# Three loads of 128 rows issued as 121 rows and 7 rows

## The chip, the cores and the metric

The kernel runs on one core of one Trainium2 chip. The metric is device time in microseconds of one execution, the median over several. A core has five engines, each with its own instruction queue: TensorE (PE, matmuls, with its weight loads PEld), VectorE (DVE), ScalarE (ACT), GpSimd (POOL) and SyncE (SP), which here only issues transfers. Transfers are carried out by 16 DMA engines. TensorE writes to eight PSUM banks, and the other engines copy the results out.

## What is computed

Sigmoid attention over 8 batches of 12 heads, 448 positions and 64 columns, then a token-mixing MLP over the joined heads:

```python
scores = scale * np.matmul(q, k.transpose(0, 1, 3, 2)) - np.log(S)
attn = 1.0 / (1.0 + np.exp(-scores))
attn_out = np.matmul(attn, v)
x = attn_out.transpose(0, 2, 1, 3).reshape(B, S, H * D)
wq, wk = x @ w_q, x @ w_k
W_tok = scale * np.einsum('bsd,btd->bst', wq, wk)
mixed = np.einsum('bst,btd->bsd', W_tok, x)
out = np.maximum(mixed, 0.0) @ w_out
```

q, k and v are float32 in HBM, 11 MB each; the output is 11 MB.

## The kernel before

The 12 heads of a batch are taken four at a time, a *quad*, so there are 24 quads, numbered in order. One quad needs one load each of q, k and v: a float32 tile of 128 rows by 896 columns, 448 KB. For v, and for q and k of some quads, a row is two pieces of 1792 B; for q and k of the other quads of the first 14 it is one piece of 3584 B. Each tile is cast to bf16 (mostly on POOL: `cast1`, lines 201, 218 and 224), q and k are brought into transposed order (on PE, or by POOL copies in `arrange`, lines 163 to 169, and DVE transposes, lines 254 to 285), and then come per quad seven score blocks on PE (line 328), seven sigmoids on ACT (line 333) and seven value blocks on PE (line 350). The MLP of a batch follows its three quads and is interleaved with later quads.

The order is written out by hand. A string `PLAN` has one letter for each step of PE with what hangs on it. A list `ORDER` has the order of the loads, and of the casts that follow them. Around the three loads in question it reads

```python
"... k4 q4 v2 w0 k5 q5 w1 v3 W5 v4 q6 k6 w4 k7 v5 q7 v6 q8 k8 k9 q9 v7 q10 v8 k10 ..."
```

(`k5` is k of quad 5; `w0` is the load of the MLP's first weights, and the other `w` entries stand for weights that load through POOL's queue.) `pump_loads` issues the loads on SP's queue in this order, each into one of eight float32 tiles of the pool `ld`, as soon as the program's order of casts has released the tile eight loads back. `pump` and `cast_now` do the casts in the same order on POOL, one after the other. So a cast whose load has not landed holds all of POOL behind it. `load_wout` issues two loads of the output weights on POOL's own DMA queue, between the casts.

Besides what the tiles need, each transfer from SP's queue waits for a transfer issued before it on the same of eight completion counters (`DMAHW0` to `DMAHW7`), which go round in turn. In this place that is the one eight transfers back.

Lines that matter below: 171 to 194 (`load1`: the two `dma_start`, profiled as lines 177 and 188), 201 (cast of q or k into the arranged order), 218 (cast of v), 278 and 254 (DVE transposes of q and k), 302 to 316 (DVE copies out of the PE transposes), 401 (a DVE copy of the MLP's input), 670 (the output weights).

Of the kernel before, what the change touches and what calls it, by code (L numbers as in the profile page):

```python
# [17 lines left out]
def kernel(  # L18
# [17 lines left out]
    P = 128  # L36
    NI, NP = 7, 64
# [112 lines left out]
    SRC = dict(q=q, k=k, v=v)  # L150
# [3 lines left out]
    def arrange(n, eng):  # L154
# [12 lines left out]
        for g in range(2):  # L167
            lo = slice(64 * g, 64 * g + 32)
            eng.tensor_copy(out=w[lo, 1], in_=z[lo])  # L169

    def load1(n, nm, eng):
        u, j = quads[n]
        if KIND[n] in "cer" and nm != "v":
            t = p_ld.tile([P, 2 * RUN + PAD], F32, tag="ld", name=nm + "32")
            t = t[:, 0 : 2 * RUN] if n < SPLIT else t.rearrange("p (y x) -> p y x", y=2)[:, :, 0:RUN]
            rows = SRC[nm][u, 4 * j : 4 * j + 4]
            eng.dma_start(
                out=t,
                in_=rows.rearrange("h (p r) d -> (h p) (r d)", r=2 * NI)
                if n < SPLIT else rows.rearrange("h (p y r) d -> (h p) y (r d)", y=2, r=NI),  # L180
            )
            ld[nm, n] = (
                t.rearrange("p (y i e d) -> p e y i d", y=2, i=NI, e=2)
                if n < SPLIT else t.rearrange("p y (i e d) -> p e y i d", i=NI, e=2)
            )
            return
        t = p_ld.tile([P, 2, NI * HD], F32, tag="ld", name=nm + "32")
        eng.dma_start(
            out=t,
            in_=SRC[nm][u, 4 * j : 4 * j + 4].rearrange(  # L190
                "(g h) (p i) d -> (h p) g (i d)", g=2, i=NI
            ),
        )
        ld[nm, n] = t

# [486 lines left out]
    def cols(r):  # L682
# [9 lines left out]
        out=ident, in_=ident, compare_op=ALU.not_equal, fill=1.0, base=0,  # L692
# [35 lines left out]
    def pump_loads():  # L728
        while len(loaded) < len(ORDER):

            late = len(ring) > LATE
            if late and not allowed[0]:
                break
            nm, n = ORDER[len(loaded)]
            if nm == "w" and n or (nm, n) in CASTING:
                loaded.add((nm, n))
                continue
            if len(ring) >= 8 and ring[-8] not in cast:
                break
            allowed[0] -= late  # L740
            ring.append((nm, n))
            if nm == "w":
                load_weights()
            else:
                load1(n, nm, nc.sync)
            loaded.add((nm, n))
# [81 lines left out]
    for t in PLAN:  # L828
# [17 lines left out]
        elif kind == "P":  # L846
            n, i = divmod(c, NI)
# [17 lines left out]
        elif t == "z":  # L865
            n = quads_r.pop(0)
# [16 lines left out]
        elif kind == "M":  # L883
            u, x = divmod(c, NC // 2)
# [48 lines left out]
```

## Time and profile before

| What | Time or share |
|---|---|
| median of 3 runs | 182.57 us |
| lowest and highest run | 180.17 and 185.29 us |
| span of the profiled execution | 180.1 us |
| ACT, line 333, the sigmoids | 140.0 us busy, 168 of them, 948 ns each |
| PE, line 328, the scores | 62.2 us busy |
| PE, line 350, the values | 47.3 us busy |
| POOL, line 201, casts of q and k | 43.2 us busy, 36 of them |
| mean rate of all transfers | 263 GB/s |

The span goes from the first to the last instruction of one execution, the one that was profiled; nothing further of that execution's own time is given, and the runs are other executions. The slices on the profile's page are 1/40 of the span, about 4.5 us each; a digit is a busy share in tenths. In the lists of waits a row names the engine and line that waited, what it waited for, the total in microseconds, how often, and the longest. In the rows on single tiles the three numbers are minimum, median and maximum; "DMA to landing" is the time from the issue of a transfer until all its data has arrived. In rows of the chain and of a timeline the first number is the start and the second the duration.

### The profile page before, as it was taken

To read this page: it belongs to the slowest core of one execution; us is meant where nothing else is said; L and a number is where in the kernel's file an instruction comes from. 1 tells how busy PE (TensorE), PEld (TensorE's weight loads), DVE (VectorE), ACT (ScalarE), POOL (GpSimd) and SP (SyncE) were. 2 spreads that over 40 slices of the span, in tenths; PEclk is the share of its full clock that TensorE was granted. 3 is DMA by queue.
4 is the path that set the end of the run, shared out by engine and by line. 5 is a ranking of instruction groups with operands and counts; after the bars stand their busy time and mean duration, and the time that the engine had idled before them with its cause. 6 is when DMAs were issued, how large, how long until landed. Compare 5 with 4: busy or idle time off the path is not lost.

```text
span 180.1 us, 7907 instructions
## 1 busy us (share of the span) xinstructions
PE 169.6 (94%) x3440; PEld 112.2 (62%) x3440; DVE 145.6 (81%) x227; ACT 159.0 (88%) x208; POOL 121.4 (67%) x166
## 2 busy tenths in 40 slices
PE   7698899889899999999999999999999999999990
PEld 3334445444575555445667786678887788888660
DVE  3578899997989896889999999979898886768351
ACT  4699999999899999999999999999999989976300
POOL 1028799689999999999999999979979910010000
PEclk9999999999999999999999999999999999999999
DMA  5999999999999998899998889987795523505876
GB/s 177 355 372 349 322 383 381 280 302 356 342 294 349 339 265 267 217 319 365 343 300 315 217 288 305 342 322 213 200 338 173 135 64 73 137 4 122 201 208 175
DMA packets 27475, 47.31 MB, mean 263 GB/s; under 512 B 3888, under 2 KB 23600, under 8 KB 27440
## 3 DMA queue, kind: packets, MB, share of 16 engines
q1 hardware_dynamic: 26160, 44.64, 78.0%
q0 software_dynamic: 800, 1.18, 3.6%
q10 hardware_dynamic: 480, 0.98, 1.5%
q8 instruction: 27, 0.44, 1.0%
q14 instruction: 8, 0.07, 0.1%
HBM read 35.78 MB, written 11.01 MB: 260 GB/s over the span
## 4 chain that ended last, share of the span: by engine, by line
PE 56%; POOL 16%; DMA 15%; DVE 5%; ACT 2%; issue 2%; SPq 1%; POOLq 0%
PE banks L539 15%; PE banks L350 10%; PE banks L328 10%; PE banks L620 8%; DMA q<-in_q_dram 6%; POOL qk L201 5%; DMA w<-in_moe_w_k_dram 4%; DMA k<-in_k_dram 3%; POOL qk L169 3%; DMA wout<-wout 2%; ACT at L333 2%; POOL v L218 2%; PE banks L579 2%; PE banks L413 2%; POOL swap L163 2%
## 5 line engine op out<-in xcount | busy, mean ns | idle before, releaser
L333 ACT ACTIVATE at<-banks 128x896 bf16<-128x896 f32 x168 | 140.0, 948 | 3.4 <-PE banks L328 3.0
L328 PE MATMUL banks<-qk 64*64 64x448 bf16 x672 | 62.2, 358 | 3.3 <-ACT at L333 1.6
L350 PE MATMUL banks<-at,v 64*64 64x448 bf16 x672 | 47.3, 351 | 0.8 <-ACT at L333 0.7
L328 PEld LDWEIGHTS <-qk 64*64 64x64 bf16 x672 | 25.9, 105 | 20.7 <-issue 13.2
L539 PE MATMUL banks<-wout,mx 64*64 64x384 bf16 x672 | 36.6, 323 | 0.0
L201 POOL CAST qk<-k 128x896 bf16<-128x896 f32 x19 | 22.8, 1199 | 10.6 <-DVE qk L302 9.7
L350 PEld LDWEIGHTS <-v 64*64 64x64 bf16 x672 | 23.2, 107 | 8.6 <-issue 1.7
L539 PEld LDWEIGHTS <-mx 64*64 64x64 bf16 x672 | 23.3, 107 | 4.5 <-issue 0.5
L359 DVE CAST xt<-banks 128x896 bf16<-128x896 f32 x22 | 23.8, 1083 | 2.3 <-PE banks L350 1.8
L620 PE MATMUL banks<-wout,mx 128*128 128x384 bf16 (+1 forms) x138 | 24.4, 320 | 0.0
L480 DVE TENSOR_SCALAR mx<-banks 128x1024 bf16<-128x1024 f32 (+3 forms) x22 | 21.3, 972 | 1.9 <-PE banks L493 0.7
L201 POOL CAST qk<-q 128x896 bf16<-128x896 f32 x17 | 20.4, 1198 | 2.6 <-DMA q<-in_q_dram 1.3
L218 POOL CAST v<-v 128x896 bf16<-128x896 f32 x22 | 20.6, 950 | 1.4 <-DMA v<-in_v_dram 0.4
L620 PEld LDWEIGHTS <-mx 128*128 128x128 bf16 x138 | 12.3, 98 | 9.8 <-issue 3.2
L285 DVE STREAM_TRANSPOSE qk<-qk 128x448 f32<-128x448 f32 x28 | 17.0, 627 | 0.4 <-POOL qk L166 0.3
L163 POOL COPY swap<-qk 32x448 uint32<-32x448 uint32 x28 | 15.5, 554 | 2.3 <-DVE qk L201 0.7
L166 POOL COPY qk<-qk 32x448 uint32<-32x448 uint32 x28 | 15.8, 566 | 1.6
L169 POOL COPY qk<-swap 32x448 uint32<-32x448 uint32 x28 | 15.8, 564 | 1.6
L254 DVE STREAM_TRANSPOSE qk<-qk 32x448 f32<-32x448 f32 x24 | 15.3, 636 | 0.6
L422 POOL COPY wq<-wqk 64x448 bf16<-64x448 bf16 x3 | 1.7, 555 | 15.7 <-DVE wqk L421 15.7
L653 DVE COPY o<-banks 128x384 f32<-128x384 f32 x12 | 6.6, 553 | 5.7 <-PE banks L620 5.3
L653 ACT COPY o<-banks 128x384 f32<-128x384 f32 x9 | 4.4, 490 | 7.1 <-PE banks L620 6.9
(91 smaller groups left out, 206.5 us busy)
## 6 DMA issues: line engine op xcount, KB each, us to landing
q<-in_q_dram SPq DMA_DIRECT2D x24, 448.0 KB, 6.6
v<-in_v_dram SPq DMA_DIRECT2D x24, 448.0 KB, 6.3
k<-in_k_dram SPq DMA_DIRECT2D x23, 448.0 KB, 7.0
out_dram<-o SPq DMA_DIRECT2D x50, 192.0 KB, 3.9
wout<-in_moe_w_out_dram POOLq DMA_DIRECT2D x2, 576.0 KB, 12.2
wout<-wout SPq DMA_DIRECT2D x12, 96.0 KB, 6.2
out_dram<-o ACTq DMA_DIRECT2D x4, 192.0 KB, 3.5
k<-in_k_dram SPq DMA_DIRECT2D x1, 256.0 KB, 5.6
```

The source lines that it names most:

```text
L163: eng.tensor_copy(out=z[lo], in_=w[hi, 0])
L169: eng.tensor_copy(out=w[lo, 1], in_=z[lo])
L201: COPY[e](out=f[:, :, "qk".index(nm)].rearrange("p e i d y -> p e y i d"), in_=ld.pop((nm, n)),)
L218: COPY[e](out=t16.rearrange("p b i d -> p (b i d)"), in_=ld.pop((nm, n)).rearrange("p b x -> p (b x)"),)
L285: nc.vector.transpose(out=qk[n][:, t].rearrange("p t i n -> p (t i n)").bitcast(F32), in_=w)
L328: nc.tensor.matmul(sc[HALF[h], g, 0:S], qk[n][HALF[g], h, 1, i, :], qk[n][HALF[g], h, 0].rearrange("p i n -> p (i n)"), start=True, stop=True,
L333: inst = nc.scalar.activation(at, sc[:, :, 0:S], ACTF.Sigmoid, bias=attn_bias, scale=attn_scale)
L350: nc.tensor.matmul(ps[HALF[g], h, 0:S], ld["v16", n][HALF[h], g, i, :], ats[n, i][HALF[h], g, :], start=(i == 0), stop=(i == NI - 1),)
L359: read(fb, COPY[eng](out=xt(u, j)[:, :, 0:S], in_=ps[:, :, 0:S]))
L480: inst = nc.vector.tensor_scalar(dst, ps, moe_scale, 0.0, ALU.mult, ALU.max)
L539: nc.tensor.matmul(ps[HALF[x], y, 0:NB], mx[HALF[y], u, b, 64 * (i - 3 * y) : 64 * (i - 3 * y) + 64], wout16[HALF[y], slot(y, b), x * NB : ...
L620: nc.tensor.matmul(ps, mxs[w][:, 2 * S * c + m * P : 2 * S * c + (m + 1) * P], wout16[:, c, w0:w1], start=(c == 0), stop=(c == NC - 1),)
```

## The change

A helper `load_rows` issues a load as it was, or, if it is one of `k5`, `v5` and `v6`, as two transfers: rows 0 to 120, then rows 121 to 127. Tiles, casts, `PLAN` and `ORDER` stay as they are.

```diff
+    THIN = "k5 v5 v6".split()
+    CUT = 121
+
+    def load_rows(nm, n, eng, dst, rows):
+
+        if f"{nm}{n}" not in THIN:
+            eng.dma_start(out=dst, in_=rows)
+            return
+        for r in (slice(0, CUT), slice(CUT, P)):
+            eng.dma_start(out=dst[r], in_=rows[r])
+
     def load1(n, nm, eng):
...
-            eng.dma_start(
-                out=t,
-                in_=rows.rearrange("h (p r) d -> (h p) (r d)", r=2 * NI)
+            load_rows(
+                nm, n, eng, t,
+                rows.rearrange("h (p r) d -> (h p) (r d)", r=2 * NI)
                 if n < SPLIT else rows.rearrange("h (p y r) d -> (h p) y (r d)", y=2, r=NI),
             )
...
-        eng.dma_start(
-            out=t,
-            in_=SRC[nm][u, 4 * j : 4 * j + 4].rearrange(
-                "(g h) (p i) d -> (h p) g (i d)", g=2, i=NI
-            ),
+        load_rows(
+            nm, n, eng, t, SRC[nm][u, 4 * j : 4 * j + 4].rearrange("(g h) (p i) d -> (h p) g (i d)", g=2, i=NI),
         )
```

SP's queue from v of quad 5 to q of quad 9, before; a row has the line, the tile written and its source, the shape, and what it waits for (`DMAHW` are the eight completion counters):

```order
L188 DMA v_444<-in_v_dram 128x2x448 [waits DMAHW7_49,Pool_49]
L177 DMA q_478<-in_q_dram 128x896 [waits DMAHW0_49,Pool_49]
L188 DMA v_481<-in_v_dram 128x2x448 [waits DMAHW1_49,Pool_49]
L177 DMA q_486<-in_q_dram 128x896 [waits DMAHW2_49,Pool_49]
L177 DMA k_504<-in_k_dram 128x896 [waits DMAHW3_49,Pool_49]
L177 DMA k_662<-in_k_dram 128x896 [waits DMAHW4_49,Pool_49]
L177 DMA q_666<-in_q_dram 128x896 [waits DMAHW5_49,Pool_49]
```

The same place after:

```order
L180 DMA v_445<-in_v_dram 121x2x448 [waits DMAHW0_49,Pool_49]
L180 DMA v_445<-in_v_dram 7x2x448 [waits DMAHW1_49]
L177 DMA q_480<-in_q_dram 128x896 [waits DMAHW2_49,Pool_49]
L180 DMA v_483<-in_v_dram 121x2x448 [waits DMAHW3_49,Pool_49]
L180 DMA v_483<-in_v_dram 7x2x448 [waits DMAHW4_49]
L177 DMA q_489<-in_q_dram 128x896 [waits DMAHW5_49,Pool_49]
L177 DMA k_507<-in_k_dram 128x896 [waits DMAHW6_49,Pool_49]
L177 DMA k_665<-in_k_dram 128x896 [waits DMAHW7_49,Pool_49]
L177 DMA q_669<-in_q_dram 128x896 [waits DMAHW0_49,Pool_49]
```

Two transfers more stand there. The last row, q of quad 9, waited for counter 5, last used by q of quad 6; it now waits for counter 0, last used by the 121 rows of v of quad 5.

POOL's queue at the casts of quad 7 before (line 434 is a copy of the MLP, line 163 begins `arrange`):

```order
L434 COPY wq_119<-wqk_117 64x448 [waits DVE_49,Pool_49]
L201 CAST qk_781<-k_438 128x2x2x224 [waits DMAHW6_49,Pool_49]
L218 CAST v_785<-v_444 128x896 [waits DMAHW7_49,PE_49]
L201 CAST qk_781<-q_478 128x2x2x224 [waits DMAHW0_49]
L163 COPY swap<-qk_781 32x448 [waits Pool_49]
```

And after; the lines below the helper stand 8 further down in the file:

```order
L442 COPY wq_119<-wqk_117 64x448 [waits DVE_49,Pool_49]
L209 CAST qk_784<-k_439 128x2x2x224 [waits DMAHW7_49,Pool_49]
L226 CAST v_788<-v_445 128x896 [waits DMAHW1_49,DMAHW0_49,PE_49]
L209 CAST qk_784<-q_480 128x2x2x224 [waits DMAHW2_49]
L163 COPY swap<-qk_784 32x448 [waits Pool_49]
```

The instructions and their order are the same; the cast of v of quad 5 waits for two counters in place of one.

## The prediction

> **What bounds the kernel now.** I read the page first, for shares and slices, then the busy time by stretches around the three loads, then the waits in the same place, the chain of waits, and the landing times of single loads.
>
> ```profile
> span 180.1 us, 7907 instructions
> ...
> PE 169.6 (94%) x3440; PEld 112.2 (62%) x3440; DVE 145.6 (81%) x227; ACT 159.0 (88%) x208; POOL 121.4 (67%) x166
> ...
> DMA  5999999999999998899998889987795523505876
> ...
> q1 hardware_dynamic: 26160, 44.64, 78.0%
> ...
> q8 instruction: 27, 0.44, 1.0%
> ```
>
> TensorE is busy 94% of the span, and DMA is at nine tenths or more for the first 70 us. The last line shows 27 instruction packets of 0.44 MB / 27 = 16 KB; each took 0.010 x 16 x 180.1 / 27 = 1.07 us. A packet lies on one DMA engine alone, so some engine is later than its fifteen neighbours. The rows do not say which one.
>
> ```profile
> 24.00:30.00 6.00, 5.85 (x90) 3.24 (x89) 5.76 (x10) 6.00 (x8) 5.93 (x7) 1.00 1.06 385
> 30.00:36.00 6.00, 5.44 (x125) 2.81 (x120) 5.76 (x9) 6.00 (x9) 4.64 (x6) 1.00 1.10 304
> 36.00:42.00 6.00, 5.25 (x147) 3.06 (x135) 5.82 (x8) 6.00 (x9) 5.25 (x8) 1.00 1.09 302
> 42.00:48.00 6.00, 5.54 (x78) 2.22 (x74) 4.88 (x9) 6.00 (x8) 5.58 (x7) 1.00 1.05 378
> 48.00:60.00 12.00, 11.96 (x248) 8.30 (x250) 10.47 (x17) 11.52 (x15) 11.15 (x17) 1.00 1.02 324
> ```
>
> The columns are PE, PEld, DVE, ACT and POOL busy, granted clock, DMA share and GB/s. From 24 to 48 us ACT is busy all the time: it is the bound there. After 48 us PE is. Nothing that PE leaves idle before 48 us can be worth more than 24 - 5.85 - 5.44 - 5.25 - 5.54 = 1.9 us. The clock is 1.00 throughout, so it plays no part.
>
> Who waits for loads in this stretch is in the waits from 24 to 48 us:
>
> ```profile
> POOL qk L201 <- DMA q<-in_q_dram: 1.3, 1, 1.3
> DVE qk L278 <- POOL qk L201: 1.1, 1, 1.1
> PE banks L328 <- DVE xn L401: 0.5, 1, 0.5
> POOL qk L201 <- DMA k<-in_k_dram: 0.3, 1, 0.3
> POOL v L218 <- PE banks L507: 0.3, 1, 0.3
> ```
>
> The chain of waits, in order of time, joins them, and the ACT timeline has its end:
>
> ```profile
> 24.57 1.22 POOL qk L201
> 25.80 10.47 DMA q<-in_q_dram
> 36.33 1.21 POOL qk L201
> ...
> 42.15 2.32 POOL qk L201 x2
> 44.49 1.17 DVE qk L278 x2
> ...
> 46.17 0.60 DVE xn L401
> ```
> ```profile
> 34.11 0.93 POOL L218 CAST v<-v 128x896 bf16<-128x896 f32 x1 [0.29 <-PE banks L507]
> ```
> ```profile
> 48.65 13.22 ACT L333 ACTIVATE at<-banks 128x896 bf16<-128x896 f32 x16 [0.48 <-PE banks L328]
> ```
>
> The q load of quad 7, issued at 25.80 us, lands 10.47 us later at 36.3; POOL waits 1.3 us for it. POOL reaches the casts of quad 8 at 42.15 and 43.3 (half of 2.32 later). DVE then waits 1.1 us for POOL, PE 0.5 us for DVE, and ACT, the bound, loses 0.48 us. So 1.3 us on POOL is 0.5 us at the end: DVE and PE hide 0.6 us of DVE's wait, and the rest is hidden before it.
>
> **The change.** Landing times of the loads concerned, in the order k of quad 5, v of quads 5 and 6, q of quads 7, 8 and 9, k of quads 8 and 9:
>
> ```profile
> L177 SPq DMA_DIRECT2D k<-in_k_dram x1: 1239/1239/1239, 15.9 to 15.9; - x1
> ...
> DMA to landing us min/median/max: 8.4/8.4/8.4
> ```
> ```profile
> L188 SPq DMA_DIRECT2D v<-in_v_dram x2: 368/368/368, 24.5 to 26.9; - x2
> ...
> DMA to landing us min/median/max: 9.5/11.0/12.5
> ```
> ```profile
> L177 SPq DMA_DIRECT2D q<-in_q_dram x3: 328/340/341, 25.8 to 31.3; - x3
> ...
> DMA to landing us min/median/max: 10.5/13.0/14.5
> ```
> ```profile
> L177 SPq DMA_DIRECT2D k<-in_k_dram x2: 328/334/340, 29.5 to 30.4; - x2
> ...
> DMA to landing us min/median/max: 13.4/13.8/14.2
> ```
>
> *Three more issues.* Each is 0.33 to 1.24 us of SP's queue (the rows just shown). SP computes nothing, and what it issues at 25.8 us waits 10.5 us for its turn: hidden.
>
> *Later issues.* An issue waits for the load eight places ahead of it, and the short pieces take places. The q load of quad 9, issued at 31.3, now waits for v of quad 5, which lands at 24.5 + 9.5 = 34.0: 2.7 us later. What hides it: that load lands 14.5 us after its issue, at 45.8, and k of quad 9 ahead of it in the queues only at 30.4 + 14.2 = 44.6. If the queues ran empty, those 2.7 us would show. I take nothing.
>
> *Two waits for one.* The casts of the three tiles wait for two landings. For k of quad 5 that is 15.9 + 8.4 = 24.3, and the cast starts at 24.57. The cast of v of quad 5 starts at 34.11, 0.1 us after its landing, so its 0.29 us of idle time, put down to PE, belong to that load. Behind it on POOL stand the quad 7 cast and all of the chain above.
>
> *The rows over the engines.* This is the term that counts. At 385 GB/s a load of 128 x 3584 B takes 1.19 us, one row on one of sixteen engines 0.149 us. At 304 GB/s, while the wout load shares the engines, it is 1.51 us and 0.19 us. No transfer with 121 rows is in the trace, so its price is bounded. Dealt out like the others, at most eight rows to an engine, it costs nothing. On one engine, 121 rows are 121 x 0.149 = 18.0 us in place of 1.2 us. Between these, equal shares of 121 = 11 x 11 give eleven rows each to eleven engines, and the seven rows one each to seven of them: the burdened engines then carry 12 rows for 8, five carry none. I take this middle one, because the 128-row loads advance at the rate of sixteen equal shares. At q of quad 7 two split loads are ahead: a burdened engine is later by 4 x 0.149 + 4 x 0.19 = 1.35 us, a relieved one earlier by 2.7 us. Behind the third, 2.1 us later or 4.2 us earlier.
>
> The Trainium skill, "DMA: Bandwidth & Descriptors", section "Why a DMA increments its semaphore by 16 and not by 1", states this rule: as many engines as the largest number up to 16 that divides the slowest dimension, the lowest-numbered ones. By it the piece of 121 rows runs on eleven; by the even dealing above the sum would be zero. The trace of before has no shape that could tell them apart. Its "Rules for kernel authors" advise one 128-partition transfer over two halves, which speaks against the change.
>
> *Sum, late engine among the five relieved.* q of quad 7 lands at 33.6 to 35.0 or so, POOL is free at 34.11 + 0.93 = 35.04, and the waits of 1.3 and 0.3 us are gone. Whether it lasts is decided at k of quad 8: it lands at 29.5 + 13.4 = 42.9 now, and then between 38.7 (-4.2) and 45.0 (+2.1) by whichever engine is last. In the early half POOL keeps its 1.6 us, DVE's wait goes, and 0.5 us at the end with it; in the late half nothing is left, as POOL is then held at k instead of q. I take half, -0.25 us. Against the execution's own span that is 180.1 to 179.85. The runs shown are 180.17, 182.57 and 185.29; the profiled span is near the fastest, so I set the difference on the median: 182.3 us. Its own range is 180.7 (all 1.9 us of PE's idle time) to 183.
>
> **The rivals.**
>
> *Late engine among the burdened.* k of quad 5 +0.6 us, q of quad 7 at 36.3 + 1.35 = 37.6, so POOL is 1.3 us later there. k of quad 8 lands at 42.9 + 2.1 = 45.0, against POOL at 43.3 + 1.3 = 44.6, so POOL is 1.7 us later. DVE, PE and ACT already wait, so all of it arrives: +1.7 us, 184.3 us. For it: eleven of sixteen engines get more rows. Against it: being late comes from work beside the rows, and it grows as the software queue works (landings from 8.4 to 12.5 us), so the late engine need not be like the rest. I put the two nearly even, with a lean to relief.
>
> The page just named, section "Latency and other measured facts", has engines 7 and 15 usually slower, with the software queue as its best guess: the one would get eleven rows, the other none. No row here can test it.
>
> *Fewer engines also run slower* (the other side). If engines that get rows dealt differently get in each other's way by a factor f, the burdened are late at k of quad 8 by 12 x 0.149f - 1.19 + 2 x (12 x 0.19f - 1.51) = 6.35f - 4.2 us. POOL has 43.3 - 42.9 = 0.4 us of slack, so slower by 2% (3.65 us) begins at f = 1.3. The nearest row is the fall from 385 to 304 GB/s, f = 1.27, when another queue's rows come in: it gives 6.35 x 1.27 - 4.2 - 0.4 = 3.5 us, 186.1 us. At f = 1.5 it is 187.5. Against it: on fewer engines the sixteen-engine total has room.
>
> *All on one engine.* 16.8 us more for k of quad 5 and 121 x 0.19 - 1.5 = 21.5 us for each v, 60 us at k of quad 8, and later loads have rows on that engine too: about 240 us. Only if 121 rows cannot be shared at all.
>
> *The split does nothing.* Even dealing, issues hidden: 182.6 us.
>
> **How the numbers follow.** Relief 0.42, burden 0.32, nothing 0.09, slower engines 0.13, one engine 0.04. The predicted time is that of relief, 182.3. The low end, 179.8, takes all of PE's 1.9 us and 0.9 us of the spread of the runs; the high end, 186.4, takes in burden and slower engines up to f = 1.3. Two per cent, 3.65 us, is about what a measurement of this kernel can tell from no change. Slower by that: one engine and most of the slower engines, 0.13. Faster: only relief with more waiting in slow runs than in the profiled one, 0.05. Within: 0.82.
>
> **What would show it.** Relief: POOL's wait for q of quad 7 and DVE's for POOL near 44 us are gone, and q lands before 35.1. Burden: that q lands near 37.6, k of quad 8 near 45, DVE's wait grows to about 2.8 us. Slower engines: k of quad 8 past 47 us, and GB/s from 24 to 42 us well below 385 and 304. Nothing: landings as now. The prediction is wrong if the landings do not move, or move and the end does not follow DVE's wait, or if SP's queue runs dry behind the short pieces.

## The result and the profile after

| | median | lowest to highest | runs |
|---|---|---|---|
| before | 182.63 us | 180.17 to 185.29 us | 6 |
| after | 186.93 us | 185.44 to 188.18 us | 6 |

The ratio is 1.029, with a 95% interval of 1.024 to 1.034: slower, by 4.3 us at the medians. Here and below, ratios leave out the runs more than 1.5% above the fastest of their kernel, while medians are of all runs: before, that leaves out 183.16 and 185.29 us, and the means then lie 5.2 us apart. The profiled execution of the changed kernel took 187.69 us, with a span of 185.8 us. So 1.9 us of a time lie outside the span, and the span of 180.1 us before belongs to a time of about 182 us, the median, not to the fastest run as the prediction had it.

From the page after: span, busy shares, granted clock in slices, the transfers of SP's queue, and the sigmoids with ACT's idle time before them (lines stand eight further down than before).

```profile
span 185.8 us, 7911 instructions
...
PE 170.6 (92%) x3439; PEld 112.4 (61%) x3440; DVE 144.8 (78%) x227; ACT 159.8 (86%) x208; POOL 121.9 (66%) x166
...
PEclk9999998799999999999999999999999999999999
...
q1 hardware_dynamic: 26166, 44.64, 78.0%
...
L341 ACT ACTIVATE at<-banks 128x896 bf16<-128x896 f32 x168 | 140.6, 940 | 8.0 <-PE banks L336 7.3
```

The busy times have hardly moved. SP's queue has six packets more than the 26160 of before, with the same bytes: that is what three loads give if an engine posts one completion packet for each transfer, 3 x (11 + 7) in place of 3 x 16. Two transfers on all sixteen engines would have given 48 more. That fits eleven and seven engines, and loads alone below show the eleven. Where time was lost is in the stretches. First one of before that was not shown, 20 to 24 us, then those of after (PE, PEld, DVE, ACT, POOL busy, clock, DMA share, GB/s):

```profile
20.00:24.00 4.00, 3.35 (x72) 1.96 (x63) 3.77 (x6) 4.00 (x6) 2.68 (x5) 1.00 1.07 352
```
```profile
20.00:24.00 4.00, 3.35 (x68) 2.10 (x64) 3.89 (x6) 4.00 (x6) 2.11 (x4) 1.00 1.09 227
24.00:30.00 6.00, 5.02 (x66) 2.30 (x58) 5.74 (x10) 6.00 (x9) 4.65 (x7) 1.00 1.05 346
30.00:36.00 6.00, 5.29 (x60) 2.25 (x61) 2.86 (x5) 3.41 (x5) 5.55 (x7) 0.72 1.07 269
36.00:42.00 6.00, 5.13 (x127) 2.90 (x124) 5.91 (x8) 5.87 (x9) 1.50 (x3) 1.00 1.11 265
42.00:48.00 6.00, 4.22 (x93) 2.28 (x88) 3.88 (x6) 4.56 (x7) 5.58 (x9) 1.00 1.01 307
48.00:60.00 12.00, 10.76 (x208) 7.01 (x211) 9.71 (x18) 10.86 (x14) 11.45 (x15) 1.00 1.02 314
```

While k of quad 5 is moved, the rate is 227 GB/s in place of 352, with the engines as busy as ever (1.09). From 30 to 42 us, with v of quads 5 and 6, it is 265 to 269 in place of 302 to 304. ACT, full before, has 2.6 us of idle time from 30 to 36 us and 1.4 us from 42 to 48 us.

POOL's timeline after, with what ended the idle time before each cast:

```profile
23.11 2.19 POOL L777 CAST wqk<-w 64x384 bf16<-64x384 f32 x4 [1.75 <-DMA w<-in_moe_w_k_dram]
26.53 1.21 POOL L209 CAST qk<-k 128x896 bf16<-128x896 f32 x1 [1.24 <-DMA k<-in_k_dram]
...
39.24 0.94 POOL L226 CAST v<-v 128x896 bf16<-128x896 f32 x1 [3.05 <-DMA v<-in_v_dram]
41.63 1.21 POOL L209 CAST qk<-q 128x896 bf16<-128x896 f32 x1 [1.46 <-DMA q<-in_q_dram]
```

The cast of k of quad 5 starts 2.0 us later than before (24.57), that of v of quad 5 5.1 us later (34.11), that of q of quad 7 5.3 us later (36.33). PE and ACT take it up in three places:

```profile
30.65 0.76 PE L358 MATMUL banks<-at,v 64*64 64x448 bf16 x12 [1.47 <-POOL v L226]
```
```profile
31.80 0.92 ACT L341 ACTIVATE at<-banks 128x896 bf16<-128x896 f32 x1 [0.81 <-PE banks L336]
34.49 11.68 ACT L341 ACTIVATE at<-banks 128x896 bf16<-128x896 f32 x14 [1.78 <-PE banks L336]
47.62 4.30 ACT L341 ACTIVATE at<-banks 128x896 bf16<-128x896 f32 x5 [1.44 <-PE banks L336]
52.58 0.92 ACT L341 ACTIVATE at<-banks 128x896 bf16<-128x896 f32 x1 [0.66 <-PE banks L336]
```

At 30 us PE waits for a v cast, that of quad 3, which stands on POOL behind k of quad 5. Its granted clock is 0.72 as a mean from 30 to 36 us, 0.50 from 32 to 34 us, and ACT loses 0.81 + 1.78 us. The later losses come through DVE:

```profile
45.33 0.65 DVE L293 STREAM_TRANSPOSE qk<-qk 128x448 f32<-128x448 f32 x1 [2.12 <-POOL qk L166]
49.81 1.17 DVE L286 STREAM_TRANSPOSE qk<-qk 128x448 f32<-128x448 f32 x2 [1.64 <-POOL qk L209]
```
```profile
46.60 0.65 PE L628 MATMUL banks<-wout,mx 128*128 128x384 bf16 x3 [1.62 <-DVE xn L409]
```

ACT's 1.44 us at 47.6 us go back to quad 7: its q is cast at 41.63, POOL's copies that arrange it hold up DVE until 45.33, and PE and ACT follow. The 0.66 us at 52.6 us are the loss that the prediction spoke of, by way of the casts of quad 8 and DVE at 49.81; it was 0.48 us before.

### The profile page after: what moved, and what is told of

The parts are those of the page before. It is cut to its first block, busy times and chain, and to the rows that moved or that the text cites. A ratio compares the mean times of both kernels' runs of the same rounds, so it can differ in the third digit from the quotient of the medians.

```text
span 185.8 us, 7911 instructions
## 1 busy us (share of the span) xinstructions
PE 170.6 (92%) x3439; PEld 112.4 (61%) x3440; DVE 144.8 (78%) x227; ACT 159.8 (86%) x208; POOL 121.9 (66%) x166
## 4 chain that ended last, share of the span: by engine, by line
PE 62%; DMA 17%; ACT 7%; POOL 5%; SPq 3%; issue 2%; DVE 1%; POOLq 0%
PE banks L547 15%; PE banks L358 12%; PE banks L336 12%; DMA k<-in_k_dram 10%; PE banks L628 9%; DMA q<-in_q_dram 7%; ACT at L341 6%; PE banks L587 3%; POOL qk L209 3%; SPq L177 2%; PE banks L421 2%; PE banks L433 2%; PE banks L380 2%; PE banks L396 2%; PE banks L501 1%
## 5 line engine op out<-in xcount | busy, mean ns | idle before, releaser
L358 PE MATMUL banks<-at,v 64*64 64x448 bf16 x672 | 48.1, 355 | 2.0 <-POOL v L226 1.5
L547 PE MATMUL banks<-wout,mx 64*64 64x384 bf16 x672 | 36.3, 323 | 0.0
L547 PEld LDWEIGHTS <-mx 64*64 64x64 bf16 x672 | 22.8, 107 | 4.4 <-issue 0.3
L430 POOL COPY wq<-wqk 64x448 bf16<-64x448 bf16 x3 | 1.7, 557 | 15.7 <-DVE wqk L429 15.7
```

The costliest lines, as they stand in the source:

```text
L358: nc.tensor.matmul(ps[HALF[g], h, 0:S], ld["v16", n][HALF[h], g, i, :], ats[n, i][HALF[h], g, :], start=(i == 0), stop=(i == NI - 1),)
L547: nc.tensor.matmul(ps[HALF[x], y, 0:NB], mx[HALF[y], u, b, 64 * (i - 3 * y) : 64 * (i - 3 * y) + 64], wout16[HALF[y], slot(y, b), x * NB : ...
```

## The experiments

The question was why a row of a split load takes longer. Three theories: *issues*, the further transfers and their turn of the counters; *burden*, twelve rows on some engines in place of eight; and *place*, that engines which write into the same part of SBUF hold each other up, whatever their number. The first expectations say *rate* for a row that takes longer, by the number of engines or by the place. All kernels but the two with loads alone are the kernel with the three loads cut in another way.

| Cut of the three loads | ratio to before | 95% interval |
|---|---|---|
| 121 and 7 rows | 1.029 | 1.024 to 1.034 |
| the same, measured again | 1.025 | 1.020 to 1.031 |
| by columns, 128 rows each | 1.007 | 1.003 to 1.011 |
| 112 and 16 rows | 1.018 | 1.010 to 1.026 |
| 112 and 16 rows, on another chip | 1.019 | 1.013 to 1.024 |
| 64 and 64 rows, halves | 1.022 | 1.014 to 1.031 |
| 120 and 8 rows | 1.025 | 1.016 to 1.035 |
| 64 and 64 rows, even and odd | 1.0005 | 0.997 to 1.004 |
| 121 and 7, k of quad 5 alone | 1.008 | 1.003 to 1.012 |
| 121 and 7, v of quads 5 and 6 alone | 1.017 | 1.008 to 1.025 |

**By columns.** Sixteen equal shares, but six transfers for three as in the change.

```diff
-        for r in (slice(0, CUT), slice(CUT, P)):
-            eng.dma_start(out=dst[r], in_=rows[r])
+        for y in range(2):
+            if len(dst.shape) == 3:
+                eng.dma_start(out=dst[:, y], in_=rows[:, y])
+            else:
+                c = slice(y * RUN, (y + 1) * RUN)
+                eng.dma_start(out=dst[:, c], in_=rows[:, c])
```

> The same three loads as two transfers each, cut by columns: 128 rows by half the columns. Sixteen equal shares as before, but the same three further issues and the same turn of the completion counters as with 121 and 7 rows. Theory issues (the further transfers and the later waits on counters make SP late and the queues run dry): slower by 4 us or so, 186 to 187 us. Theory burden (some engines carry 12 rows for 8): as before, 182 to 183 us. Theory rate (a row takes longer when a transfer is dealt over eleven and seven engines): as before, 182 to 183 us, packets of 1792 B at 74 to 79 ns from 20 to 24 us.

Measured 182.56 against 181.48 us, 0.7% slower. *Issues* falls as the main cause, as 0.7% is a quarter of the loss; what of the 0.7% is the issues and what the shorter pieces of k of quad 5 (1792 B in place of 3584 B) was not separated.

**112 and 16 rows; 64 and 64; 120 and 8.** One number changes each time.

```diff
-    CUT = 121
+    CUT = 112
```

> Cut after row 112: both parts divide by 16, seven rows and one row to each of sixteen engines. Issues: 186 to 187 us. Burden: no engine carries more, 182 to 183 us. Rate, if it comes from the number of engines: 182 to 183 us; rate, if it comes from where in SBUF the engines' shares fall (seven rows each are not the same places as eight): slower, 184 to 187 us, and 3584 B packets above 200 ns from 20 to 24 us.

> Cut after row 64: four and four rows to each of sixteen engines, but each part fills one half of SBUF's rows. Issues: 186 to 187 us. Burden: 182 to 183 us. Rate by the number of engines: 182 to 183 us. Rate by the place in SBUF: sixteen engines write into one half at a time, slower by as much as 121 and 7 or more, 186 to 190 us, with packets near twice their 148 and 77 ns.

> Cut after row 120: fifteen engines with eight rows and eight of them with one more; one engine with none. Issues: 186 to 187 us. Burden: an engine carries one row more a load, 0.5 us at k of quad 8 in place of 2.1 us; 182.5 to 183.5 us, and 182 us if the one without rows was the late one. Rate by the number of engines: a little, 183 to 184 us. Rate by the place in SBUF: depends on whether eight rows in a block fall like the sixteen shares of 128 rows; 182.5 if they do, up to 187 if not.

Medians 184.43, 185.98 and 186.65 us, against 181.48. With 112 and 16 and with 64 and 64 rows every engine carries the eight rows it had (SP's queue has 26208 packets in both, 48 more than before, which is sixteen engines in every part), and the time is lost all the same. *Burden* cannot be the main cause. Nor can the number of engines. The halves were to cost as much as 121 and 7 rows or more; at 1.022 they came out lower, with intervals that overlap. The stretches 20 to 24 and 30 to 36 us of the cut into halves, and below of the cut by columns:

```profile
20.00:24.00 4.00, 3.31 (x88) 1.82 (x81) 3.36 (x6) 4.00 (x6) 1.95 (x4) 1.00 1.10 222
...
30.00:36.00 6.00, 5.62 (x96) 2.96 (x88) 5.82 (x9) 6.00 (x9) 4.71 (x6) 1.00 1.09 256
```
```profile
20.00:24.00 4.00, 3.53 (x92) 2.13 (x92) 3.37 (x5) 4.00 (x6) 3.08 (x5) 1.00 1.08 332
...
30.00:36.00 6.00, 5.58 (x96) 3.15 (x96) 5.80 (x11) 6.00 (x9) 5.89 (x7) 1.00 1.10 304
```

222 and 256 GB/s against 332 and 304, with the engines about equally busy: a row takes longer.

**Even and odd rows.** As many rows and transfers as the cut into halves, with the same waits; only which rows go together differs.

```diff
-        for r in (slice(0, CUT), slice(CUT, P)):
+        for r in (slice(0, P, 2), slice(1, P, 2)):
```

> The kernel, the three loads as 64 even rows and 64 odd rows: as many rows to a transfer and as many transfers as in the cut after row 64, four rows to each of sixteen engines. Place in SBUF: both halves reach all of SBUF, so near the cut by columns, 182 to 183.5 us, packets of 3584 B near 150 ns from 20 to 24 us. If any transfer of other than 128 rows is slow: as the cut after row 64, 185 to 187 us.

Measured 181.74 against 181.88 us: nothing is lost. Its stretches:

```profile
20.00:24.00 4.00, 3.38 (x89) 2.00 (x88) 3.33 (x7) 3.95 (x6) 3.13 (x6) 1.00 0.96 319
...
30.00:36.00 6.00, 5.67 (x93) 2.84 (x89) 5.83 (x9) 6.00 (x9) 5.89 (x8) 1.00 1.10 305
```

This pair is the clearest of the study. Six transfers for three cost nothing here that the runs could tell (0.4% at most), and 64 rows to a transfer cost nothing, when every second row of SBUF is taken.

**Loads alone.** Nothing but loads, to part SBUF from HBM: `sb` and `hb` are the steps between rows in SBUF and in HBM, `n` the rows, `m` the packets of a row.

```python
for n, m, sb, hb in PHASES:
    for i, t in enumerate(T):
        src = flat[256 * i : 256 * (i + 1)].rearrange("(m p) x -> p m x", m=2)[0 : n * hb : hb, 0:m]
        nc.sync.dma_start(out=t[0 : n * sb : sb, 0:m, 0:X], in_=src)
    settle()
```

> Only loads, none of the computation: ten stretches of twelve loads from q into SBUF in packets of 3584 B, each stretch begun when the one before is over. By stretch: 128 rows; 121; 120; 112; 96; then 64 rows of two packets each, with the rows in SBUF next to each other or every second one, and the rows in HBM likewise (both next to each other; SBUF every second; HBM every second; both every second); 128 rows again. Theory place in SBUF: the two stretches that fill every second row of SBUF run near the rate of 128 rows, the two that fill 64 rows next to each other run near half, whatever is done in HBM; 121, 120 and 112 rows run at 220 to 270 GB/s against 390 to 400. Theory place in HBM: it is the HBM side that decides. Theory burden: 120, 112, 96 and 64 rows run within 7% of the rate of 128 rows and 121 at 11/16 of it, 270 GB/s, with packets as short as in 128 rows (140 to 150 ns).

The stretches in order, without the first, in which DVE was still clearing the tiles: 121, 120, 112, 96 rows; 64 next to each other; 64 every second one in SBUF; 64 every second one in HBM; both; 128 rows. The columns after the length are DVE and POOL busy, clock, DMA share, GB/s.

```profile
29.20:58.60 29.40, 1.69 (x11) 0.00 (x0) 1.00 0.68 177
60.30:82.50 22.20, 1.69 (x11) 0.00 (x0) 1.00 0.95 233
84.40:100.80 16.40, 1.69 (x11) 0.00 (x0) 1.00 0.99 294
102.50:118.60 16.10, 1.69 (x11) 0.00 (x0) 1.00 0.97 256
120.90:148.00 27.10, 1.69 (x11) 0.00 (x0) 1.00 1.01 203
150.70:166.40 15.70, 1.69 (x11) 0.00 (x0) 1.00 0.95 351
168.50:195.60 27.10, 1.69 (x11) 0.00 (x0) 1.00 1.00 203
197.80:214.00 16.20, 1.69 (x11) 0.00 (x0) 1.00 0.92 341
215.70:231.60 15.90, 1.69 (x11) 0.00 (x0) 1.00 0.91 345
```

64 rows next to each other in SBUF get 203 GB/s, 64 spread rows 341 to 351, as 128 rows do (345). Whether the rows are spread in HBM makes no difference to the first (203 and 203) and little to the second. The transfers of SP's queue in the fifth, the sixth and the first of these stretches (packets, MB, share of 16 engines):

```profile
q1 hardware_dynamic: 1728, 5.51, 100.6%
```
```profile
q1 hardware_dynamic: 1728, 5.51, 94.9%
```
```profile
q1 hardware_dynamic: 1583, 5.20, 68.3%
```

A packet takes 1.006 x 16 x 27.1 / 1728 = 252 ns next to each other, 0.949 x 16 x 15.7 / 1728 = 138 ns spread, and 0.683 x 16 x 29.4 / 1583 = 203 ns with 121 rows, where 68% is eleven engines of sixteen. These are means over all packets, the small ones of completion with them, one in nine to twelve. So 121 rows lose twice: on eleven engines, and by packets half as long again. For the halves *place* stands, and its place is SBUF. That the long packets of 121 rows have the same cause is likely, but no run spread 121 rows in another way. *Burden* had 270 GB/s for 121 rows, with short packets; measured were 177.

The Trainium skill, "SBUF — State Buffer", section "Door 1: The DMA port swizzle (why `[64,N]` ≈ `[32,N]`)", states that a transfer's rate depends on how many of 16 ports its partitions reach, and that 64 partitions in a row reach half of them. The rows are near it: 203 of 351 GB/s, a little over half.

**Loads alone, other shapes.** To see uneven shares without a clash, and how the clash follows from the number of rows.

```diff
-    (128, 1, 1, 1), (121, 1, 1, 1), (120, 1, 1, 1), (112, 1, 1, 1), (96, 1, 1, 1),
-    (64, 2, 1, 1), (64, 2, 2, 1), (64, 2, 1, 2), (64, 2, 2, 2), (128, 1, 1, 1),
+    (128, 1, 1, 1), (88, 1, 1, 1), (104, 1, 1, 1), (64, 2, 2, 1), (44, 2, 2, 1),
+    (55, 2, 2, 1), (32, 2, 4, 1), (32, 2, 1, 1), (121, 1, 1, 1), (128, 1, 1, 1),
```

> Only loads again, none of the computation, ten stretches of twelve: 128 rows; 88 and 104 rows next to each other (by even shares eight rows on eleven and on thirteen engines); 64 rows, every second one of SBUF, two packets each; 44 rows, every second one, two packets (four rows on eleven engines, in the same blocks as the 64); 55 rows, every second one, two packets (five rows on eleven engines); 32 rows, every fourth one, two packets; 32 rows next to each other, two packets; 121; 128. Uneven shares without a clash of places is 44 rows: packets at 140 ns and 11/16 of the rate of the 64 rows, 240 GB/s. If fewer engines themselves made packets slow, its packets are at 200 ns or more. 55 rows has the same engines in other blocks: with a clash, packets over 170 ns. 88 and 104 rows: packets at 140 ns if 128 rows too are dealt in blocks of eight, over 200 ns if 128 rows are dealt in another way. 32 rows next to each other: half the rate, 203 GB/s, if they reach as many ways into SBUF as 64 rows, a quarter if every way serves its own rows.

In order from the second: 88; 104; 64 every second one; 44 and 55 every second one; 32 every fourth one; 32 next to each other; 121; 128 rows.

```profile
29.20:45.30 16.10, 1.69 (x11) 0.00 (x0) 1.00 0.64 235
47.00:68.70 21.70, 1.69 (x11) 0.00 (x0) 1.00 0.82 206
71.30:86.60 15.30, 1.69 (x11) 0.00 (x0) 1.00 0.96 359
89.10:108.30 19.20, 1.69 (x11) 0.00 (x0) 1.00 0.67 196
110.70:131.30 20.60, 1.70 (x11) 0.00 (x0) 1.00 0.69 230
133.60:143.90 10.30, 1.65 (x11) 0.00 (x0) 1.00 0.84 267
145.60:159.00 13.40, 1.54 (x10) 0.00 (x0) 1.00 1.00 204
161.10:188.40 27.30, 1.69 (x11) 0.00 (x0) 1.00 0.69 191
190.10:205.60 15.50, 1.69 (x11) 0.00 (x0) 1.00 0.95 355
```

88 rows are the case of uneven shares alone: DMA share 0.64, 235 GB/s, 11/16 of the 345 to 355 of 128 rows being 237 to 244, and 140 ns a packet by the working above. Fewer engines need not make a packet longer. 32 rows next to each other get the same 204 GB/s as 64, more than half of 345 to 355 and not a quarter. The Trainium skill, "SBUF — State Buffer", in the section just named, states that 32 partitions in a row reach as many ports as 64; the rows agree. But the expectation for 44 rows failed, 196 GB/s and 175 ns in place of 240 and 140, and so did the one that blocks of eight rows are free: 104 rows get 206 GB/s, with 203 ns. By which rule rows are dealt to engines when a transfer is not on all sixteen, and so which counts clash, stays open.

**How much the uneven shares add.**

> 121 and 7 rows once more, on one chip with the cut after row 112, to size what the uneven shares add. 1.025 to 1.033 of before.

> 112 and 16 rows once more beside it. Theory place alone: within 0.5% of 121 and 7 rows. Place and burden: 0.7 to 1.3% faster than 121 and 7 rows, at 1.015 to 1.02 of before.

187.16 and 185.99 us on one chip, 1.025 and 1.019 of before: 0.6% apart, with intervals that overlap. With no engine carrying more rows, 112 and 16 rows have three quarters of the loss at these point ratios (0.019 of 0.025) and under two thirds in the first pair (0.018 of 0.029). That the rest is burden is not shown: the rows themselves clash differently, 112 rows alone taking 169 ns a packet (0.988 x 16 x 16.4 / 1536) where 121 rows take 203.

**k of quad 5 alone, and the two v loads alone.** The second run has `"v5 v6"` in the same line.

```diff
-    THIN = "k5 v5 v6".split()
+    THIN = "k5".split()
```

> 121 and 7 rows for k of quad 5 alone. The load lands 1.8 to 2 us late, at 26.3 us, and everything behind it, but the queues have until q of quad 7 to catch up. Theory place: q of quad 7 lands 1 to 2 us late, 183 to 184.5 us. Theory burden: 0.6 us late, 182 to 182.7 us.

> 121 and 7 rows for v of quads 5 and 6 alone. Theory place: k of quad 8 lands 3 us late and POOL, DVE and ACT with it, 184 to 185.5 us; together with the run of k of quad 5 alone the differences add up to those of all three. Theory burden: 1.5 us late, 183 to 184 us.

182.92 and 185.07 us against 181.88: 0.8% and 1.7%, together 2.4%, near the 2.5 to 2.9% of all three. Both parts reach the end, and the two v loads weigh about twice what the k load does at these ratios. k of quad 5 alone comes out between its two forecasts.

## Why the prediction was wrong

*What bounds the kernel, and the path.* Right in the main. ACT bounds the stretch, POOL stands behind the loads in order, and lateness of POOL at quad 8 goes through DVE and PE to ACT. But that is the smallest of three places: ACT lost 2.6 us after 30 us, by way of v of quad 3, and 1.4 us by way of quad 7, which the prediction did not have. It also gave the clock no part, as it was 1.00 before. The landings after of q of quads 7 and 8, and of k of quads 8 and 9:

```profile
L177 SPq DMA_DIRECT2D q<-in_q_dram x2: 351/354/357, 27.8 to 31.0; - x2
DMA to landing us min/median/max: 13.8/14.8/15.7
```
```profile
L177 SPq DMA_DIRECT2D k<-in_k_dram x2: 328/340/351, 32.7 to 34.6; - x2
DMA to landing us min/median/max: 14.3/14.7/15.0
```

q of quad 7 lands at 27.8 + 13.8 = 41.6 us (36.3 before), k of quad 8 at 32.7 + 15.0 = 47.7 (42.9 before). That is the prediction's own sign of slower engines, k of quad 8 past 47 us. But POOL comes to that cast only at 48.58 and does not wait for it: q of quad 7 had already made POOL late. Of the 5.3 us of q of quad 7, 2.0 are a later issue, at 27.77 in place of 25.80, since each time it goes out when the cast of k of quad 5 ends; 3.3 are a longer way to landing, 13.8 in place of 10.5 us. The prediction had only the second kind.

*The issues and the counters.* Right, nearly nothing: by even and odd rows 0.05%, with an interval of 0.4% to each side. q of quad 9 was issued late, at 38.6 us in place of 31.3, and its cast at 50.83 waits for nothing: hidden, as said.

*Eleven and seven engines.* Right, by the six packets; and in loads alone twelve transfers of 121 rows show 131 packets under 512 B in their stretch, eleven for each but one, where those of 64 rows show 192, sixteen for each.

*The price of a row.* This is the step that failed: "The rows over the engines" priced a row of the split loads at 0.149 and 0.19 us, the rate of sixteen equal shares, for any share an engine is given. In the runs that rate held for 128 rows, for rows spread over SBUF on sixteen engines and for 88 rows in a block on eleven, and not for the other shapes tried. What SP's queue moved from 20 to 24 us, before and after:

```profile
q1 hardware_dynamic: 1036, 1.39, 105.2%
```
```profile
q1 hardware_dynamic: 687, 0.89, 106.4%
```

1.052 x 16 x 4 / 1.39 = 48.4 us of engine time for a MB became 1.064 x 16 x 4 / 0.89 = 76.5, a factor f of 1.58; it is a mean over all that the queue moved, weights and whole loads too. By the same working even and odd rows keep 48.4 (0.960 x 16 x 4 / 1.27), and the halves have 79.8 (1.085 x 16 x 4 / 0.87). Put into the prediction's own sum for slower engines, 1.58 gives 6.35 x 1.58 - 4.2 = 5.8 us at k of quad 8; measured were 4.8, with its issue 3.2 us later.

*The choice among the cases.* Relief of a late engine had 0.42 and was taken; q of quad 7 was to land before 35.1 us. Any relief was lost in the slower rows. "Fewer engines also run slower", with 0.13, was the mechanism that came: f = 1.58 lies beyond its threshold of 1.3, and 2.9% beyond its 2%. Its name had the wrong cause, though: 112 and 16 rows and the halves lose on all sixteen engines, and even and odd rows do not, so there it is not how many engines write but where. The reason given against it, that the total has room, was no argument about places.

*Cover that was not there.* k of quad 5 was given 0.6 us in the burden case and taken no further. POOL had nothing to spare between it and the v cast of quad 3 behind it: both start 2.0 us late, and PE waits 1.47 us for that cast at 30 us. In the run of k of quad 5 alone that cast is only 0.5 us late (28.14 for 27.69), ACT has no idle time at 30 us, and its 0.8% come at quads 7 and 8 (0.73 + 0.64 us).

*The range.* 179.8 to 186.4 us missed 186.93 by half a microsecond. It stopped at f = 1.3, though the text had a value for f = 1.5, 187.5 us; loads alone show up to 252 for 138 ns, which is 1.8.

How much of the loss is PE's lower clock and how much the waits before it was not separated. In the profile of the changed kernel when measured again it comes elsewhere:

```profile
30.00:36.00 6.00, 5.43 (x88) 2.83 (x89) 4.65 (x8) 5.00 (x7) 5.37 (x7) 1.00 1.09 255
42.00:48.00 6.00, 3.17 (x32) 0.96 (x18) 2.84 (x4) 2.70 (x4) 5.58 (x10) 0.77 1.02 336
```

There ACT loses 1.0 us from 30 to 36 us at a clock of 1.00, and 3.3 us from 42 to 48 us, where the clock is 0.50 in the last two. The span is much the same, 185.5 and 185.8 us.

## What to carry to other kernels

Cut a load into interleaved rows (which cost nothing here) or by columns (0.7%), not into blocks of rows: a block of 64 rows moves at 203 GB/s where 64 spread rows or all 128 move at 341 to 359. Before giving some DMA engines fewer rows, price what the others do with theirs at up to 1.8 times the time of a packet (252 for 138 ns), not at the old rate; and remember that a slow transfer also slows the loads beside it in the queues, here the weights issued before it (POOL's wait for them went from 0.8 to 1.75 us).

## What the runs showed of the hardware

A transfer of 121 rows runs on eleven engines and one of 7 rows on seven. Packets of 3584 B, completion packets counted in, took 138 ns on average spread over SBUF and 252 ns when sixteen engines wrote into 64 rows next to each other, with the steps in HBM without influence. 88 rows, on eleven engines, kept packets of 140 ns; blocks of 121, 120, 112, 104 and 96 rows moved at 177, 233, 294, 206 and 256 GB/s, where 128 rows moved at 345. And PE's granted clock was 0.50 from 32 to 34 us, where before that only a wait of 1.47 us stood out; that the one caused the other was not tried.
